# Transposed values in contiguous columns, nine stored weight blocks, two pairs coupled on TensorE, and a new order

## The chip, the cores and the metric

The kernel runs on one core of a Trainium2 chip. The metric is the device time of one execution in microseconds. One core has five engines that each run their own instruction stream: TensorE (PE, with its weight loads shown apart as PEld), VectorE (DVE), ScalarE (ACT), GpSimd (POOL) and SyncE (SP, which here does nothing but issue DMAs). Work on one engine stands in a fixed order; semaphores tie the engines together.

## The reference

Three stages follow each other. The first is a linear recurrence over 768 time steps for 4 x 8 heads of 40 x 40 state; the second and third are dense layers over 3072 tokens.

```
for t in range(768):                       # for each of 4 x 8 heads
    y[t]  = r[t] @ state
    Sa    = state @ a[t]
    state = state * w[t] - outer(Sa, b[t]) + outer(v[t], k[t])
x   = y as [3072 tokens, 320]
x2  = max(x@w1, x@w2, x@w3) @ w_out        # 320 -> 768 -> 320
out = ((x2@w_a) * (x2@w_b)) @ w_out2       # 320 -> 1536 -> 320
```

## The kernel before, in words

The recurrence is cut into 24 chunks of 32 steps; two chunks make a pair, of which there are 12 (p = 0 to 11). `prep(p)` loads a pair's inputs, forms running products of the decays (the scans at L433 and L437), scales the keys (L441), multiplies keys with the other inputs on PE (L484 for the first five pairs, L466 for the later ones, 16 matmuls of 64 columns each) and inverts the 32 x 32 triangular blocks of all heads (`solve`). The inverse is made of two 16 x 16 halves, and there are two ways to join them. For p < KS, `chain` joins them on PE: after the product with the halves (L685) come a product with the raw coupling block (L704), a copy, and a second product with the halves (L712). For p >= KS, `solve` multiplies the coupling block out beforehand on DVE and POOL (the products TC at L550 to L552), sends it through DRAM (ED, L528 and L530), and `chain` needs one product after L685 (L698). KS is 4.

`chain(c)` carries the state through chunk c and forms the chunk's outputs. For the outputs, the tile XT holds two transposed 80-row operands for 16 head pairs: the values v, loaded by DMA at L616, and the solved rows u, transposed on PE (L774) and copied by ACT at L777. The product at L786 then uses, for each of 16 index pairs, 64 columns of XT as the stationary operand and 64 columns of r (RB) as the moving one. Before the change, the 64 columns of one product stand 16 elements apart:

```
T.matmul(ps[...], XT[0:80, 2 * u + x::NU], RB[0:80, :, 2 * u + x], ...)      # L786
```

`moe_a(p)` runs the first dense stage for the 256 tokens of a finished pair (lines 909 to 938). Its weights come as 64-bit floats and are turned into two 32-bit parts (`pieces`, lines 834 to 872). `moe_b(n)` runs the second dense stage for 512 tokens (L1063 to L1073) after all chunks, six times. Its twelve weight blocks are also 64-bit. For the first LV blocks `stage_b` converts them during the recurrence and writes the parts to DRAM (WD), and `weights_b` reads them back once the recurrence's tiles are free; the rest are loaded and converted at that point (`live_b`). LV is 6.

The order is made by a planner (`Plan.run`), on the host, before the program exists. Every operation is recorded with an engine, an estimated duration, a priority and its dependences; the planner places the operation that can start first, by priority among those that are ready, and writes each engine's stream in that order. SLOPE, WP, SBP, GPR and MAP are priorities; XWAY, PMD, PME and PRE0 are latencies and margins. Where the plan leaves PE without work (between FT0 and FT1), it puts fillers into PE's stream: 128 x 128 matmuls on the identity (L313). They stand in the stream for good and run whether or not PE is idle then. The diff touches the constants, `Plan.run`, and in `body` the tile XT, its load, its copy and the product; `layout` orders v on the host.

Of the kernel before, what the change touches and what calls it, by code (L numbers as in the profile page):

```python
# [8 lines left out]
F32 = mybir.dt.float32  # L9
F32R = mybir.dt.float32r  # L10
U32 = mybir.dt.uint32
AF = mybir.ActivationFunctionType
# [3 lines left out]
B, H, S, D = 4, 8, 768, 40  # L16
C = 32
NCH = S // C
NP = NCH // 2
NU = 16  # L20
# [5 lines left out]
NACC = 9  # L26
LV = 6
KG = 5
KS = 4
NSPL = 2  # L30
DMIN = 0.4
NPB = 3
NH = 2
WP = 0.1
BIAS, BIASP = 0.2, -9
# [13 lines left out]
XRATE = 270e3  # L49
XWAY = 1.8  # L50
XISS = 0.46
XQ = 1.0
SLOPE = 0.6
PMD = 1.5
PME = 0
PRE0 = -0.5
EPA = 0.6
GPR = 0.0
SBP = 8.0
MAP = 2.0  # L60
MODE = 0.1


# [4 lines left out]
class Plan:  # L68
# [30 lines left out]
    def run(self, limit):  # L99
        n = len(self.ops)  # L100
# [6 lines left out]
        for o in reversed(self.ops):  # L107
# [3 lines left out]
            t = d + l + o["pre"] + o["xfer"]  # L111
# [15 lines left out]
        done, last, top = 0, 0, 0.0  # L127
        line, port, mode = 0.0, 0.0, None
        busy = {}

# [23 lines left out]
        while done < n:  # L154
            best = None
            for eng, rs in ready.items():
# [3 lines left out]
                c = []  # L160
                own = [est[i] for i in rs if len(self.ops[i]["ways"]) == 1] if eng == "DVE" else ()
                for i in rs:
                    o = self.ops[i]
                    s = max(ft, est[i] + o["pre"])
                    if o["xfer"]:
                        s = max(s, line - XQ)
                    if eng == "POOL" or isinstance(o["ways"][eng][0], Both):
                        s = max(s, port)
                    if o["ps"]:
                        kind = o["ps"][0][0]  # L170
                        if kind != "a" and fifo[kind][0] != i:
                            continue
                        if used.get(kind, 0) + len(o["ps"]) > limit[kind] or len(banks) < len(o["ps"]):
                            continue
                        s = max(s, heapq.nsmallest(len(o["ps"]), banks)[-1][0])
# [21 lines left out]
            s, i, eng = best  # L197
            o = self.ops[i]
            dur, fn, _ = o["ways"][eng]
            if eng == "PE":  # L200
# [30 lines left out]
                if not warm(s):  # L231
                    dur *= 2
                if o["md"] != mode:
                    dur += MODE if o["md"] else 0.0
                elif mode:
                    dur -= MODE
# [38 lines left out]
def body(nc, tc, ia, out_ap):  # L275
# [17 lines left out]
    def dma(fn, nbytes, r=(), w=(), pri=0.0, pre=1.2):  # L293
        return op("SP", XISS, fn, r=r, w=w, pri=pri, lat=XWAY, pre=pre, xfer=nbytes / XRATE)
# [57 lines left out]
    XU = ap_.tile([128, 4, 2, 40], F32, name="XU")  # L352
    XT = ap_.tile([128, 2 * C * NU], F32, name="XT")
    ZR = [ap_.tile([128, 2, 8, 2, 40], F32, name=f"ZR{i}") for i in range(NZR)]
# [237 lines left out]
    def chain(c):  # L592
# [19 lines left out]
        for g in range(2):  # L612
            r0 = GP[g]
            dma(lambda w_, g=g, r0=r0: SP.dma_start(RB[40 * g:40 * g + 40, g].rearrange("p u t -> p (u t)"), ia["rb"][c, g]),
                82e3, w=[("RB", g)], pri=pr, pre=4.0 if c else 1.2)
        dma(lambda w_: SP.dma_start(XT[0:80, 0:C * NU], ia["vt"][c]),  # L616
            260e3, w=[("XTv", 0), ("XTv", 1)], pri=pr, pre=4.0 if c else 1.2)
# [154 lines left out]
        def xtr(w_):  # L772
# [4 lines left out]
        i = op("ACT", ac(512), lambda w_: A.activation(  # L777
            XT[0:80, C * NU:2 * C * NU].rearrange("p (s n) -> p n s", n=NU), bank[w_[px]][0:80].rearrange("p (n s) -> p n s", s=32), AF.Copy),
            r=[px], w=[("XTu", 0), ("XTu", 1)], fin=[px], pri=0.2 + pr)
        pg = ("a", "g", c)  # L780

        def gmm(w_):
            ps = bank[w_[pg]]
            for u in range(8):
                for x in range(2):
                    T.matmul(ps[64 * x:64 * x + 64, u * 64:u * 64 + 64], XT[0:80, 2 * u + x::NU], RB[0:80, :, 2 * u + x], start=True, stop=True)  # L786

# [471 lines left out]
def layout(d):  # L1259
    f = np.float32  # L1260
    a6 = lambda z: np.asarray(z).reshape(B, 2, 2, 2, NCH, C, D)
    o = {}
# [30 lines left out]
    o["rb"] = np.ascontiguousarray(em(r)).reshape(NCH, 2, D, -1)  # L1293
    o["vt"] = np.ascontiguousarray(em(v).reshape(NCH, 2 * D, NU, C).transpose(0, 1, 3, 2)).reshape(NCH, 2 * D, -1)
    o["ry"] = np.ascontiguousarray(r.transpose(4, 2, 6, 0, 1, 3, 5)).reshape(NCH, 2, D, -1)
# [43 lines left out]
```

## Time and profile before

| | us |
|---|---|
| three timed runs | 1073.09, 1075.58, 1079.2 (median 1075.58) |
| the profiled execution | 1066.23, its span 1064.5 |
| PE busy in the span | 1033.2 (97%) |
| DVE, ACT, POOL busy | 611.2, 514.3, 136.8 |

The span runs from the first to the last instruction; 1.73 us of the profiled execution lie around it. A row of the groups gives a source line, engine, operation, tiles, shapes and count, then busy time, the mean of one, and the engine's idle time just before. An fp32 matmul of the program has up to two matmul records, so 768 records at L786 are 24 chunks of 16 matmuls, 448 at L466 are 14 calls, and 512 at L712 are 8 calls. A busy PE includes the fillers.

### The profile page before, as it was taken

How to read it: one execution, taken by the hardware profiler on the slowest of the kernel's cores; microseconds unless marked ns; L12 is line 12 of the kernel's file. 1: busy time of each engine (PE TensorE's matmuls, PEld its weight loads, DVE VectorE, ACT ScalarE, POOL GpSimd, SP SyncE). 2: the span in 40 equal slices, each digit the busy share in tenths (PEclk: the TensorE clock that was granted, in tenths of full speed). 3: DMA queues.
4: the chain of work that ended last, by engine and by line, in shares of the span. 5: the costliest groups of instructions: out<-in, count | busy, mean ns of one | idle time of the engine just before them, and what ended most of it. 6: DMA issues, size and time to landing. Idle time of an engine off the chain costs nothing.

```text
span 1064.5 us, 34992 instructions
## 1 busy us (share of the span) xinstructions
PE 1033.2 (97%) x15374; PEld 933.3 (88%) x15374; DVE 611.2 (57%) x1023; ACT 514.3 (48%) x1153; POOL 136.8 (13%) x124
## 2 busy tenths in 40 slices
PE   8999999899999989998999999999999999999997
PEld 8877888799989879897999999888888888888886
DVE  7966678877778767786773367673232232332222
ACT  4256886677577748575575333343232232222221
POOL 3200014221224013232120001000000000000000
PEclk9989999999999999999999999999999999999999
DMA  8744774745655465655633166512001000000000
GB/s 230 168 114 125 196 184 110 159 108 154 163 138 139 142 128 145 169 141 136 175 93 109 34 195 210 143 56 70 1 24 32 1 25 1 26 1 1 25 1 28
DMA packets 133134, 109.01 MB, mean 102 GB/s; under 512 B 90608, under 2 KB 107888, under 8 KB 132016
## 3 DMA queue, kind: packets, MB, share of 16 engines
q1 hardware_dynamic: 132112, 103.76, 37.8%
q8 instruction: 123, 2.02, 0.8%
q10 hardware_dynamic: 864, 2.95, 0.7%
q14 instruction: 35, 0.29, 0.1%
HBM read 82.15 MB, written 24.51 MB: 100 GB/s over the span
## 4 chain that ended last, share of the span: by engine, by line
PE 83%; DMA 6%; DVE 4%; ACT 3%; SPq 2%; issue 1%; POOL 1%; DVEq 0%; ACTq 0%; POOLq 0%
PE bank L1063 25%; PE bank L909 16%; PE bank L786 4%; PE bank L1071 4%; PE bank L1073 4%; PE bank L1072 4%; PE bank L804 3%; DMA KT<-in_kb_dram 2%; PE bank L645 2%; PE bank L313 2%; PE bank L934 2%; PE bank L628 2%; PE bank L738 2%; PE bank L671 1%; PE bank L935 1%; PE bank L466 1%
## 5 line engine op out<-in xcount | busy, mean ns | idle before, releaser
L1081 DVE TENSOR_TENSOR bas<-bank,bas 128x512 f32<-128x512 f32 x72 | 49.8, 691 | 201.9 <-PE bank L1063 194.7
L1063 PE MATMUL bank<-bxhi,bw 128*128 128x512 f32 x576 | 156.4, 393 | 0.0
L1063 PEld LDWEIGHTS bank<-bxhi,bw 128*128 128x128 f32 x576 | 106.3, 188 | 21.1
L1083 ACT ACTIVATE bgh<-bas 128x512 fp32r<-128x512 f32 x72 | 45.6, 633 | 130.8 <-DVE bas L1081 130.8
L1080 ACT ACTIVATE bas<-bank 128x512 f32<-128x512 f32 x72 | 43.1, 599 | 134.4 <-PE bank L1063 131.8
L909 PE MATMUL bank<-xhi,whi 128*128 128x256 f32 x432 | 94.5, 300 | 0.0
L1063 PE MATMUL bank<-bxlo,bw 128*128 128x512 f32 x288 | 89.8, 393 | 0.0
L1071 PE MATMUL bank<-bo,bgh 128*128 128x320 f32 x288 | 88.9, 309 | 0.0
L1073 PE MATMUL bank<-bo,bgl 128*128 128x320 f32 x288 | 88.9, 309 | 0.0
L1072 PE MATMUL bank<-bo,bgh 128*128 128x320 f32 x288 | 88.8, 308 | 0.0
L909 PE MATMUL bank<-xlo,whi 128*128 128x256 f32 x432 | 87.1, 283 | 0.0
L909 PE MATMUL bank<-xhi,wlo 128*128 128x256 f32 x432 | 87.1, 283 | 0.0
L924 DVE TENSOR_TENSOR hm<-bank,hm 128x512 f32<-128x512 f32 x72 | 49.5, 688 | 53.5 <-PE bank L909 50.5
L1084 DVE TENSOR_TENSOR bgl<-bas,bgh 128x512 fp32r<-128x512 f32 x72 | 49.8, 691 | 44.6 <-ACT bgh L1083 44.4
L909 PEld LDWEIGHTS bank<-xhi,whi 128*128 128x128 f32 x432 | 66.6, 191 | 2.8
L909 PEld LDWEIGHTS bank<-xhi,wlo 128*128 128x128 f32 x432 | 67.3, 192 | 0.0
L909 PEld LDWEIGHTS bank<-xlo,whi 128*128 128x128 f32 x432 | 67.2, 192 | 0.0
L313 PE MATMUL bank<-con 128*128 128x128 f32 x456 | 62.8, 292 | 3.3 <-DMA con<-in_con_dram 3.0
L1063 PEld LDWEIGHTS bank<-bxlo,bw 128*128 128x128 f32 x288 | 54.1, 188 | 12.4
L313 PEld LDWEIGHTS bank<-con 128*128 128x128 f32 x456 | 58.0, 204 | 5.6 <-ACT bank L382 2.9
L451 POOL TENSOR_TENSOR ZL<-ZL,Pp 64x512 f32<-64x512 f32 x28 | 40.0, 1429 | 175.9 <-DVE Pp L433 81.0
L909 PE MATMUL bank<-xt,wt 128*128 128x256 f32 x216 | 61.3, 284 | 0.5 <-POOL wt L872 0.5
(185 smaller groups left out, 2358.1 us busy)
## 6 DMA issues: line engine op xcount, KB each, us to landing
KT<-in_kb_dram SPq DMA_DIRECT2D x20, 384.0 KB
wraw<-in_wpb_dram SPq DMA_DIRECT2D x6, 960.0 KB
wraw<-in_wpa_dram SPq DMA_DIRECT2D x6, 768.0 KB
Wp<-in_wf_dram SPq DMA_DIRECT2D x20, 198.4 KB
ZR<-in_vz_dram SPq DMA_DIRECT2D x48, 80.0 KB
XX<-in_vx_dram SPq DMA_DIRECT2D x48, 80.0 KB
XT<-in_vt_dram SPq DMA_DIRECT2D x24, 160.0 KB
RB<-in_rb_dram SPq DMA_DIRECT2D x48, 80.0 KB
```

The source lines that it names most:

```text
L313: P.keep = lambda b: T.matmul(bank[b][:, 0:128], ident, ident, start=True, stop=True)
L786: T.matmul(ps[64 * x:64 * x + 64, u * 64:u * 64 + 64], XT[0:80, 2 * u + x::NU], RB[0:80, :, 2 * u + x], start=True, stop=True)
L909: T.matmul(ps, w, x, start=(i == 0), stop=(i == 7))
L924: op("DVE", dv(512, True), lambda w_, pn=pn: V.tensor_tensor(f(hm), bank[w_[pn]], f(hm), ALU.max), r=[pn], w=["hm"], fin=[pn], pri=ep)
L1063: T.matmul(ps, w, x, start=(k == 0), stop=(k == 7))
L1071: T.matmul(o, gh[:, c], oh, start=ff == 0, stop=False)
L1072: T.matmul(o, gh[:, c], ol, start=False, stop=False)
L1073: T.matmul(o, gl[:, c], oh, start=False, stop=ff == 11)
L1080: op("ACT", ac(512), lambda w_, j=j, pa=pa: A.activation(tb["as", j], bank[w_[pa]], AF.Copy), r=[pa], w=[("bas", j)], fin=[pa], pri=ep)
L1081: op("DVE", dv(512, True), lambda w_, j=j, pb=pb: V.tensor_tensor(tb["as", j], bank[w_[pb]], tb["as", j], ALU.mult), r=[pb], w=[("bas", j) ...
L1083: op("ACT", ac(512), lambda w_, j=j, k=k: A.activation(tb["gh", k], tb["as", j], AF.Copy), r=[("bas", j)], w=[("gh", k)], pri=ep)
L1084: op("DVE", dv(512), lambda w_, j=j, k=k: V.tensor_tensor(tb["gl", k], tb["as", j], tb["gh", k], ALU.subtract), r=[("bas", j), ("gh", k)], ...
```

## The change

XT becomes a tile [128, 16, 2, 32]: for each index pair the 32 values and the 32 solved rows lie next to each other, so the 64 columns of a product are contiguous. The host no longer transposes v, so that each row of the load, 512 contiguous elements before, now lands as 16 pieces of 32 elements (128 bytes). The copy at L777 writes runs of 32. LV goes from 6 to 9: three more weight blocks are converted during the recurrence, and three fewer after it. KS goes from 4 to 2: pairs 2 and 3 (chunks 4 to 7) get their coupling blocks from DVE and POOL. Six numbers of the planner change, and its model gets a limit on how fast PE's small matmuls are fetched.

```diff
--- before.py
+++ after.py
@@ -24,14 +24,14 @@
 NYR, NZR = 2, 1
 NW = 9
 NACC = 9
-LV = 6
+LV = 9
 KG = 5
-KS = 4
+KS = 2
 NSPL = 2
 DMIN = 0.4
 NPB = 3
 NH = 2
-WP = 0.1
+WP = 0.3
 BIAS, BIASP = 0.2, -9
 HOLD, HOLDP = {"DVE": 0.4, "POOL": 0.4}, 1
 OWN, WAIT = -9, 0.5
@@ -47,18 +47,19 @@
 LIMIT = 2.0 ** 100
 LAT = {"PE": 0.25, "ACT": 0.1, "DVE": 0.1, "POOL": 0.12}
 XRATE = 270e3
-XWAY = 1.8
+XWAY = 1.5
 XISS = 0.46
 XQ = 1.0
-SLOPE = 0.6
+SLOPE = 0.45
 PMD = 1.5
-PME = 0
+PME = 0.15
 PRE0 = -0.5
 EPA = 0.6
-GPR = 0.0
-SBP = 8.0
+GPR = 0.2
+SBP = 4.0
 MAP = 2.0
 MODE = 0.1
+ICAP, IRATE, IT = 400.0, 60.0, 40.0
 
 
 class Both(float):
@@ -126,6 +127,8 @@
                     ready.setdefault(e, set()).add(o["i"])
         done, last, top = 0, 0, 0.0
         line, port, mode = 0.0, 0.0, None
+        itime, ileft = 0.0, ICAP
+        count = lambda o: 0 if not o["md"] else 64 if o["md"] == "c64" and o["act"] > 0.42 else 128
         busy = {}
 
         state = [False]
@@ -166,6 +169,8 @@
                         s = max(s, line - XQ)
                     if eng == "POOL" or isinstance(o["ways"][eng][0], Both):
                         s = max(s, port)
+                    if eng == "PE" and o["md"] and s > IT:
+                        s = max(s, itime + (min(ICAP, count(o)) - ileft) / IRATE)
                     if o["ps"]:
                         kind = o["ps"][0][0]
                         if kind != "a" and fifo[kind][0] != i:
@@ -230,6 +235,8 @@
                         s += FD
                 if not warm(s):
                     dur *= 2
+                ileft = min(ICAP, ileft + (s - itime) * IRATE) - (count(o) or 16)
+                itime = s
                 if o["md"] != mode:
                     dur += MODE if o["md"] else 0.0
                 elif mode:
@@ -350,7 +357,7 @@
     YR = [ap_.tile([128, 2, 8, 2, 40], F32, name=f"YR{i}") for i in range(NYR)]
     XX = ap_.tile([128, 8, 2, 40], F32, name="XX")
     XU = ap_.tile([128, 4, 2, 40], F32, name="XU")
-    XT = ap_.tile([128, 2 * C * NU], F32, name="XT")
+    XT = ap_.tile([128, NU, 2, 32], F32, name="XT")
     ZR = [ap_.tile([128, 2, 8, 2, 40], F32, name=f"ZR{i}") for i in range(NZR)]
     ST = ap_.tile([128, 8, 2, 64], F32, name="ST")
     Zs = ap_.tile([128, 8, 40], F32, name="Zs")
@@ -613,7 +620,7 @@
             r0 = GP[g]
             dma(lambda w_, g=g, r0=r0: SP.dma_start(RB[40 * g:40 * g + 40, g].rearrange("p u t -> p (u t)"), ia["rb"][c, g]),
                 82e3, w=[("RB", g)], pri=pr, pre=4.0 if c else 1.2)
-        dma(lambda w_: SP.dma_start(XT[0:80, 0:C * NU], ia["vt"][c]),
+        dma(lambda w_: SP.dma_start(XT[0:80, :, 0, :], ia["vt"][c].rearrange("p (u t) -> p u t", t=32)),
             260e3, w=[("XTv", 0), ("XTv", 1)], pri=pr, pre=4.0 if c else 1.2)
         for x in range(2):
             y0 = 64 * (1 - x)
@@ -775,7 +782,7 @@
 
         op("PE", 0.4, xtr, r=["XU", "con"], w=[px], ps=[px], pri=0.2 + pr)
         i = op("ACT", ac(512), lambda w_: A.activation(
-            XT[0:80, C * NU:2 * C * NU].rearrange("p (s n) -> p n s", n=NU), bank[w_[px]][0:80].rearrange("p (n s) -> p n s", s=32), AF.Copy),
+            XT[0:80, :, 1], bank[w_[px]][0:80].rearrange("p (n s) -> p n s", s=32), AF.Copy),
             r=[px], w=[("XTu", 0), ("XTu", 1)], fin=[px], pri=0.2 + pr)
         pg = ("a", "g", c)
 
@@ -783,7 +790,7 @@
             ps = bank[w_[pg]]
             for u in range(8):
                 for x in range(2):
-                    T.matmul(ps[64 * x:64 * x + 64, u * 64:u * 64 + 64], XT[0:80, 2 * u + x::NU], RB[0:80, :, 2 * u + x], start=True, stop=True)
+                    T.matmul(ps[64 * x:64 * x + 64, u * 64:u * 64 + 64], XT[0:80, 2 * u + x].rearrange("p k s -> p (k s)"), RB[0:80, :, 2 * u + x], start=True, stop=True)
 
         op("PE", 1.08, gmm, md="c64", r=[("XTu", 0), ("XTu", 1), ("XTv", 0), ("XTv", 1), ("RB", 0), ("RB", 1)], w=[pg], ps=[pg], act=0.45, pri=0.2 + pr)
         for x in range(2):
@@ -1291,7 +1298,7 @@
     o["eye"] = np.zeros((128, 528), f)
     o["eye"][:, 16:].reshape(128, 16, 32)[:, :, 0:16] = np.eye(16, dtype=f)
     o["rb"] = np.ascontiguousarray(em(r)).reshape(NCH, 2, D, -1)
-    o["vt"] = np.ascontiguousarray(em(v).reshape(NCH, 2 * D, NU, C).transpose(0, 1, 3, 2)).reshape(NCH, 2 * D, -1)
+    o["vt"] = np.ascontiguousarray(em(v)).reshape(NCH, 2 * D, -1)
     o["ry"] = np.ascontiguousarray(r.transpose(4, 2, 6, 0, 1, 3, 5)).reshape(NCH, 2, D, -1)
     o["vx"] = np.ascontiguousarray(v.transpose(4, 2, 5, 0, 1, 3, 6)).reshape(NCH, 2, C, -1)
     o["vz"] = np.ascontiguousarray(v[:, :, ::-1].transpose(4, 3, 5, 0, 1, 2, 6)).reshape(NCH, 2, C, -1)
```

The lines of `before` below L47 stand 7 further down afterwards (L786 is L793, L313 is L320).

PE, chunk 4, the first of pair 2, in the stream before: the product with the halves, the coupling product (L704) and the second product with the halves (L712), with the dense stage's L909 between them.

```order
L685 MATMUL bank_67<-Zs,TT_142 32x40 x32
L909 MATMUL bank_65<-xhi,whi 128x256 x2
...
L909 MATMUL bank_65<-xl_110,wt_103 128x256
L704 MATMUL bank_66<-Zy,NB_145 32x40 x32
L909 MATMUL bank_69<-xhi,whi 128x256 x2
...
L909 MATMUL bank_69<-xl_110,wt_103 128x256
L712 MATMUL bank_67<-Zs,TT_142 32x40 x32
```

The same place in the stream after: the product with the halves, then one product with the finished coupling block (L705).

```order
L692 MATMUL bank_66<-Zs,TT_142 32x40 x32
L916 MATMUL bank_63<-xhi,whi 128x256 x2
...
L916 MATMUL bank_63<-xl_110,wt_103 128x256
L916 MATMUL bank_63<-xhi,whi 128x256 x2
...
L916 MATMUL bank_63<-xl_110,wt_103 128x256
L705 MATMUL bank_70<-Zy,NB_145 32x40 x32
```

The third product (L712, L719 after) is gone from chunks 4 to 7.

PE, where pair 4's key products (L484) stand in chunk 6, before: 12 fillers behind the second one, then the key transposes (L628).

```order
L804 MATMUL bank_67<-YL,YR_133 40x32 x32
L484 MATMUL bank_65<-ZL_128,KT_125 64x32 x32
L313 MATMUL bank_67<-con 128x128 x12
L628 MATMUL bank_67<-con,KT_126 128x104 x4
L628 MATMUL bank_65<-con,KT_126 128x104 x4
L313 MATMUL bank_64<-con 128x128 x2
```

The same pair after: 34 fillers (L320) between its two key products (L491), and 8 ahead of the product with the halves.

```order
L635 MATMUL bank_64<-con,KT_126 128x104 x4
L635 MATMUL bank_69<-con,KT_126 128x104 x4
L320 MATMUL bank_63<-con 128x128 x8
L692 MATMUL bank_63<-Zs,TT_140 32x40 x32
L491 MATMUL bank_64<-ZL_128,KT_125 64x32 x32
L320 MATMUL bank_69<-con 128x128 x34
L491 MATMUL bank_69<-ZL_128,KT_125 64x32 x32
```

Over the whole stream the fillers go from 228 to 269: 197 before and 250 after stand ahead of the eighth product at L786 (of chunk 7), 31 and 19 behind it.

SP, the loads of pair 2's coupling blocks (NB) and of one chunk's values (XT), before: NB comes straight from BD, the values as 80 x 512.

```order
L512 DMA NB_145<-BD_73 16x16x16
L609 DMA XX<-in_vx_dram 32x640 x2
L616 DMA XT<-in_vt_dram 80x512
L609 DMA ZR_137<-in_vz_dram 32x640 x2
L614 DMA RB<-in_rb_dram 40x512 x2
```

SP, the same pair after: the values as 80 x 16 x 32, and NB by way of TC and ED.

```order
L530 DMA TT_142<-TD_76 32x16x32 x4
L623 DMA XT<-in_vt_dram 80x16x32
L621 DMA RB<-in_rb_dram 40x512 x2
L427 DMA ZL_128<-in_aa_dram 48x2x512
L535 DMA ED_79<-TC 64x128 x2
L427 DMA ZL_128<-in_aa_dram 48x2x512
L627 DMA YL<-in_ry_dram 40x512 x2
L537 DMA NB_145<-ED_79 16x16x16 x3
```

The load of the values keeps its place among a chunk's loads; NB of pairs 2 and 3 moves behind the end of that pair's inverse.

## Rows read from the trace of the kernel before

**Rows 1.** The page, part 4: chain that ended last, share of the span by engine

```profile
PE 83%; DMA 6%; DVE 4%; ACT 3%; SPq 2%; issue 1%; POOL 1%; DVEq 0%; ACTq 0%; POOLq 0%
```

**Rows 2.** Stretches: start:end, length, busy us (count) of PE, PEld, DVE, ACT, POOL; clock, DMA, GB/s

```profile
0.00:73.00 73.00, 68.18 (x1076) 61.88 (x1078) 58.43 (x91) 28.91 (x73) 16.95 (x18) 0.95 0.69 173
73.00:170.00 97.00, 94.99 (x2542) 78.20 (x2543) 67.59 (x116) 71.88 (x184) 7.74 (x11) 0.96 0.64 160
170.00:260.00 90.00, 86.59 (x2044) 79.18 (x2032) 71.06 (x123) 66.49 (x161) 26.18 (x24) 1.00 0.58 139
260.00:605.00 345.00, 330.02 (x7214) 310.53 (x7214) 238.98 (x401) 217.75 (x509) 80.04 (x62) 0.99 0.51 133
605.00:664.00 59.00, 59.00 (x496) 58.83 (x495) 37.80 (x73) 20.25 (x41) 4.11 (x7) 1.00 0.63 186
664.00:1064.50 400.50, 394.38 (x2034) 344.72 (x2032) 137.31 (x222) 108.98 (x188) 1.84 (x2) 1.00 0.10 29
```

**Rows 3.** Waits of PE: line, what it waited for, us in total, times, longest us

```profile
PE bank L466 <- DVE KT L441: 5.8, 2, 4.1
PE bank L804 <- DVE YL L790: 3.6, 1, 3.6
PE bank L738 <- issue: 2.7, 3, 1.2
PE bank L786 <- ACT XT L777: 1.7, 8, 0.3
```

**Rows 4.** Groups on PE by line and shape: count, busy us, mean ns, idle before

```profile
L786 PE MATMUL bank<-RB,XT 80*64 80x64 f32 x768 | 50.1, 283 | 1.7 <-ACT XT L777 1.7
L786 PEld LDWEIGHTS bank<-RB,XT 80*64 80x64 f32 x768 | 46.8, 211 | 5.2 <-ACT XT L777 3.3 <-issue 0.3
L466 PE MATMUL bank<-ZL,KT 128*64 128x64 f32 x448 | 16.6, 230 | 6.3 <-DVE KT L441 5.8 <-issue 0.5
L466 PEld LDWEIGHTS bank<-ZL,KT 128*64 128x64 f32 x448 | 14.8, 143 | 8.4 <-issue 7.0 <-ACT YR L635 0.5
L712 PE MATMUL bank<-Zs,TT 32*32 32x40 f32 x512 | 7.1, 207 | 0.6 <-issue 0.6
L313 PE MATMUL bank<-con 128*128 128x128 f32 x456 | 62.8, 292 | 3.3 <-DMA con<-in_con_dram 3.0 <-ACT YR L656 0.4
```

**Rows 5.** The same view, lines on ACT, DVE and POOL

```profile
L777 ACT ACTIVATE XT<-bank 80x512 f32<-80x512 f32 x24 | 25.5, 1062 | 16.4 <-PE bank L774 14.4 <-DVE ST L757 1.8
L922 ACT ACTIVATE hm<-bank 128x512 f32<-128x512 f32 x36 | 21.6, 599 | 36.2 <-PE bank L909 30.5 <-POOL hlo L926 1.9 <-DVE hlo L927 1.9
L837 DVE SCALAR_TENSOR_TENSOR wraw<-wraw,wca 128x960 f32<-128x960 uint32 x6 | 6.9, 1146 | 0.0
L552 DVE TENSOR_REDUCE TC<-TP 128x64 f32<-128x512 f32 x8 | 5.4, 675 | 0.0
L550 POOL TENSOR_TENSOR TP<-BU,TU 128x512 f32<-128x512 f32 x16 | 21.9, 1385 | 64.9 <-ACT TU L586 62.4 <-DVE TC L552 2.5
```

**Rows 6.** The page, parts 2 and 3: DMA packets by size, and the main queue

```profile
DMA packets 133134, 109.01 MB, mean 102 GB/s; under 512 B 90608, under 2 KB 107888, under 8 KB 132016
q1 hardware_dynamic: 132112, 103.76, 37.8%
```

**Rows 7.** Timeline of the SP queue around one load of the values: start us, us

```profile
217.25 2.01 SPq L616 DMA_DIRECT2D XT<-in_vt_dram  x1
```

**Rows 8.** Timeline of PE, the product that needs that load: start us, us

```profile
226.69 2.05 PE L786 MATMUL bank<-RB,XT 80*64 80x64 f32 x32
```

**Rows 9.** The chain of waits around 290 us: start us, us, what

```profile
285.95 7.02 DMA KT<-in_kb_dram
293.07 1.24 DVE KT L441
294.39 1.15 PE bank L466 x32
```

## The prediction

> **What bounds the kernel now.** I began with the chain of waits as shares by engine [rows 1]: TensorE holds 83% of what ended last, DMA 6%, VectorE 4%, ScalarE 3%. The kernel is bound by TensorE's own stream, so any microsecond taken out of that stream should show nearly whole. The view by stretches [rows 2] says where. Up to 605 us the chunks run, from 605 to 664 us the first dense stage ends, and from 664 us the second dense stage runs alone. In the last stretch TensorE does 394.38 us of work in 400.5 us, and nothing in its matmuls is edited, so 400 us of the span are fixed. Ahead of it TensorE is busy 68.18 + 94.99 + 86.59 + 330.02 + 59.00 = 638.8 of 664 us; only 25 us are idle. VectorE is busy 58.43 of 73, 67.59 of 97, 71.06 of 90 and 238.98 of 345 us: high in the first 260 us, 69% later. The third view, TensorE's waits [rows 3], names little: 5.8 us in two waits for scaled keys (L441), 3.6 us for one mask, 2.7 us of issue, and 1.7 us in eight waits for the copy into XT. Others wait for TensorE far more: a single copy line, L922, stood idle 30.5 us for L909 [rows 5]. The fourth view, the groups [rows 4], shows what in TensorE's stream is dear.
>
> **The product on XT.** L786 has 768 records in 50.1 us: 24 calls of 50.1 / 24 = 2.09 us [rows 4]. L466 has the same 16 matmuls of 64 stationary and 64 moving columns, with contiguous stationary columns: 16.6 / 14 = 1.19 us a call. Their weight loads differ likewise, 211 against 143 ns. The matmuls' moving operands are laid out alike (two runs of 32), only the rows differ (80 against 128), and I take it that fewer rows don't make a product slower. So the spread columns are the cause, and contiguous ones give 24 x (2.09 - 1.19) = 24 x 0.90 = 21.6 us back. The bounds are 0 (the cause is another) and 24 x (2.09 - 1.15) = 22.6 us (one L466 call on the chain took 1.15 [rows 9]). I take 21.6.
>
> A rule of the Trainium skill speaks against it: "TensorE: Matmul & The Clock Gate", section "LDWEIGHTS (loading the stationary operand)", has a load's time follow from the number of columns alone, and both lines load 64; by that rule this term would be 0. The trace does not agree with it here, 211 against 143 ns at equal columns. "SBUF — State Buffer", section "Door 1: The DMA port swizzle (why `[64,N]` ≈ `[32,N]`)", says that fp32 accesses more than four elements apart pay for each new line, and the elements here stand 16 apart; with it the trace agrees.
>
> **The copy into XT.** L777 takes 1062 ns and writes single elements 64 bytes apart; L922 copies as many columns in 599 ns into contiguous space [rows 5]. The copy should drop to about 0.6 us, 24 x 0.46 = 11 us of ScalarE. ScalarE is not the bound; what reaches TensorE is at most the 1.7 us of the eight waits [rows 3]. I count 0 to 1.7 and take 0.
>
> **The load of the values.** 24 loads of 80 rows become 24 x 1280 pieces. The main queue's 132112 packets took 37.8% of 16 engines' 1064.5 us [rows 6], which is 6438 us or 48.7 ns a packet on the mean. A load then takes 1280 x 48.7 / 16 = 3.9 us instead of 0.9 (160 KB at the 186 GB/s of the fifth stretch [rows 2]). The net 28800 packets are 28800 x 48.7 / 16 = 88 us of all 16 engines, which lifts their share ahead of 605 us from a weighted mean of 0.56 [rows 2] by 0.15. The loads have room: one was issued at 217.25 us and its product began at 226.69 us [rows 7, 8], 9.4 us later. Its cost at TensorE is 0 with that cover, and up to 24 x 3.0 = 72 us if it is gone everywhere; near the first row I take 0.
>
> **Three more stored blocks.** Each is converted in six passes over 128 x 960; the longest kind takes 1.15 us [rows 5], so at most 6.9 us a block and 20.7 us for three, on VectorE or in part on GpSimd, moved from behind 605 us to ahead of it. It lands in the later chunks, where VectorE goes from 69% to at most (238.98 + 20.7) / 345 = 75%. Behind 605 us VectorE loses as much, where TensorE never waited: 59.00 of 59 us busy. The bytes read after the recurrence stay the same (stored parts are as long as the raw 64-bit block). Cost 0, covered by TensorE's own work; without cover up to 20.7. I take 0, since VectorE's idle time there is 106 us.
>
> **Coupling of pairs 2 and 3.** Four chunks lose L712, 7.1 / 8 = 0.89 us a call [rows 4]: 4 x 0.89 = 3.6 us out of TensorE's stream. In exchange each pair gets three products and three sums over 512 elements: 0.675 us a sum, and 0.675 to 1.385 us a product by engine [rows 5], 3 x 1.35 to 3 x 2.06 = 4.1 to 6.2 us a pair, in the first 260 us where VectorE is busiest. Its coupling block now waits for TC and a trip through ED. Behind the ED store on SP's queue stand a load of the next pair's inputs, the loads of r and the weights of the first dense stage; behind L698 on TensorE stand the state update and all that follows. The plan puts fillers there, and these are the price I count.
>
> **Fillers.** The streams hold 228 before and 269 after. L313 was busy 62.8 us, 62.8 / 228 = 0.275 us each, so 41 more cost 11.3 us. Twelve fewer stand behind chunk 7 and 53 more ahead of it; there they take 14.6 us of what the first chunks gain. They run whether needed or not, so 11.3 is firm unless they stand where TensorE would have waited anyway, which the waits [rows 3] show for 25 us at most.
>
> **The rest of the order.** It can take back some of the 25 us of waits or add to them. A faster L786 leaves the other engines less lead. The nearest row is the pair of waits for scaled keys, 5.8 us. Bounds: -12 (half of all idle goes) to +15 (each of ten pairs waits 1.5 us more). I take +3, half of that row.
>
> **Sum.** -21.6 - 3.6 + 11.3 + 3 = -10.9. The profiled execution is 1066.2 us, 9.4 us under the median of the runs; I take the difference as the same on either, so 1066.2 - 10.9 = 1055.3 there and 1075.6 - 10.9 = 1064.7 by the median. I forecast 1064.5.
>
> **Rivals.** *All of it arrives.* The new order takes waits back as well: -21.6 - 3.6 + 11.3 - 12 = -26, 1050. For it: the planner counts L786 as long as L466, so the order before was made for a faster product than the chip had, and now fits. Against: TensorE has only 25 us of idle to win.
>
> *The first chunks eat it.* Up to 260 us VectorE runs at up to 80% (58.43 of 73, then 71.06 of 90) [rows 2], and takes 8 to 12 us of new products; the 53 fillers mark where the plan itself sees TensorE wait. If these chunks lengthen by the whole 12 us, -10.9 + 12 = +1, 1076: no change. Against: VectorE's work there is hidden wherever dense work fills TensorE.
>
> *The DMA engines become the bound (slower).* The place is the keys' load. In the chain it landed 7.02 us after issue, the scaling followed at once and TensorE's L466 right behind it [rows 9], so what delays that load delays TensorE. The load of the values, 3.9 us of all engines, goes through the same queue in every chunk. If it pushes the keys' load of all ten later pairs back by 3.0 us, it costs 30 us: -10.9 + 30 = +19, 1095; if of half, 15: 1080. It decides from 11 us on, about 1.1 us a pair. For it: the share is 0.69 and 0.64 in the first stretches. Against: only two of ten pairs waited for keys. "DMA: Bandwidth & Descriptors", section "Specifications", of the Trainium skill puts the piece for full rate at 512 bytes or more; the pieces are 128. That 90608 of 133134 packets are under 512 bytes already [rows 6] agrees with pieces being usual here, and no run yet shows their price.
>
> *The change doesn't do what it says.* If L786 stays at 2.09 us for another reason, nothing gives the other engines less lead either, and the sum is -3.6 + 11.3 = +7.7, 1083. For it only that the rows differ, against it two like products in one trace. The rule on columns cited above would have it so.
>
> **How the numbers follow.** Forecast 0.50 (its own range 1058 to 1070), all arrives 0.20 (1046 to 1058), first chunks 0.15 (1070 to 1081), DMA 0.11 (1080 to 1095), no effect 0.04. The range that should hold 8 of 10 reaches from 1047 to 1080. What a measurement here can tell from no change is 0.5%, 5.4 us: faster is under 1070.2, same up to 1081. Faster: nearly all of the forecast, 0.48, the second case 0.20 and a little of the third 0.02, 0.70. Same: 0.13 + 0.02 + 0.02 = 0.17. Slower: 0.13.
>
> **What would show it.** In the profile after, L793 (the old L786) at about 28.5 us in all and its weight loads near 143 ns; L784 (the old L777) near 0.6 us; fillers at 74 us; L719 with 256 records; waits of TensorE under 30 us ahead of the second dense stage, which starts 10 us or so earlier and lasts as long. I am wrong if L793 keeps 2 us a call, if waits for keys, for XT or for coupling blocks grow past 15 us together, or if the granted clock, 0.95 and 0.96 in the first two stretches, falls in the later ones.

## Result: 2.6% faster, some two and a half times the forecast gain

The changed kernel takes 1044.66 us (median of four runs, 1041.81 to 1049.88); the kernel before, run beside it, 1074.93 (four runs, 1073.09 to 1079.2). The ratio on record is 0.9736, with an interval of 0.9697 to 0.9775 (the two medians alone give 0.972). Forecast were 1064.5 and a range of 1047 to 1080. The profiled execution of the changed kernel took 1043.9 us, span 1042.0, mean granted clock 0.995; that of the kernel before 1066.23, 1064.5 and 0.989.

In the profile after, first the page: busy time by engine, DMA packets by size, the main queue, and the chain's shares.

```profile
span 1042.0 us, 34646 instructions
PE 1011.2 (97%) x15200; PEld 913.6 (88%) x15200; DVE 623.5 (60%) x1014; ACT 501.7 (48%) x1143; POOL 140.8 (14%) x115
...
DMA packets 165180, 115.01 MB, mean 110 GB/s; under 512 B 121632, under 2 KB 140704, under 8 KB 164064
...
q1 hardware_dynamic: 163728, 108.31, 42.0%
...
PE 90%; DMA 3%; ACT 2%; DVE 2%; issue 2%; POOL 1%; SPq 1%; POOLq 0%; DVEq 0%
```

TensorE is bound as before, its share of the chain higher (83% in [rows 1]). Its busy time fell by 22.0 us, its idle time by 0.5 (1064.5 - 1033.2 = 31.3 to 1042.0 - 1011.2 = 30.8): the span's 22.5 us lie in busy time.

The groups of the changed lines (busy us, mean ns of one, then idle time before them) show in which:

```profile
L320 PE MATMUL bank<-con 128*128 128x128 f32 x538 | 70.8, 285 | 5.9 <-DMA con<-in_con_dram 2.9 <-ACT Zs L684 1.6 <-DVE YL L797 0.7
...
L793 PE MATMUL bank<-RB,XT 80*64 80x64 f32 x768 | 28.0, 225 | 0.5 <-issue 0.5
L793 PEld LDWEIGHTS bank<-RB,XT 80*64 80x64 f32 x768 | 24.6, 138 | 3.4 <-issue 0.7
...
L784 ACT ACTIVATE XT<-bank 80x512 f32<-80x512 f32 x24 | 14.3, 594 | 13.0 <-PE bank L781 12.2 <-ACT YR L642 0.5
...
L719 PE MATMUL bank<-Zs,TT 32*32 32x40 f32 x256 | 3.2, 199 | 0.0
```

The product (L793, L786 before) went from 50.1 to 28.0 us and its weight loads from 211 to 138 ns [rows 4]; the copy into XT from 1062 to 594 ns [rows 5]; the third products (L719, L712 before) from 7.1 to 3.2 us. The 269 fillers (538 records) take 70.8 us instead of 62.8. That is -22.1 - 3.9 + 8.0 = -18.0 of the 22.0 us.

The remaining 4 us can't be put down to a line: busy times of neighbouring groups overlap, and the other groups together fall by 1.6 us only. The stretches show what else differs. The columns are those of [rows 2]; the last but two is the granted clock.

```profile
0.00:73.00 73.00, 69.92 (x1247) 62.59 (x1248) 62.20 (x100) 32.36 (x84) 15.35 (x17) 1.00 0.75 185
73.00:170.00 97.00, 92.95 (x2396) 77.16 (x2394) 75.89 (x125) 75.85 (x196) 19.61 (x17) 1.00 0.66 162
170.00:260.00 90.00, 88.73 (x1940) 82.98 (x1942) 81.58 (x126) 60.32 (x151) 33.28 (x27) 1.00 0.64 144
260.00:589.00 329.00, 312.99 (x7161) 294.18 (x7159) 247.16 (x414) 210.87 (x503) 71.20 (x54) 0.99 0.61 151
589.00:642.00 53.00, 53.00 (x441) 52.70 (x441) 19.55 (x34) 13.36 (x24) 0.00 (x0) 1.00 0.78 226
642.00:1042.00 400.00, 393.59 (x2029) 343.99 (x2028) 137.12 (x220) 108.90 (x188) 1.31 (x1) 1.00 0.10 28
```

Where [rows 2] had a granted clock of 0.95 and 0.96 in the first two stretches, it is 1.00 now. The second dense stage is the same 400 us and begins 22 us earlier, where some 10 were forecast.

**Time and clock apart.** Each run lists its mean granted clock. The runs of the kernel before spread with it: over 40 of them, a line through time against clock falls by 9.0 us for each 0.01 of clock. Time multiplied by clock (below: the net time) is thus a fair reading of what the kernel would take at full clock, and time less net of what it loses to the clock. It is an estimate, good to some 2 us over a difference of 0.01, where it takes 10.7 us and the line 9.0; it counts a low clock as lost even while TensorE waits, where it costs nothing. It shows already that the profile I worked from, at 0.989, was a fast execution of the kernel before; its other runs had 0.983 on the mean.

### The profile page after: what moved, and what is told of

Same layout as the page of the kernel before. It is cut to its first block, busy times and chain, and to the rows that moved or that the text cites. A ratio compares the mean times of both kernels' runs of the same rounds, so it can differ in the third digit from the quotient of the medians.

```text
span 1042.0 us, 34646 instructions
## 1 busy us (share of the span) xinstructions
PE 1011.2 (97%) x15200; PEld 913.6 (88%) x15200; DVE 623.5 (60%) x1014; ACT 501.7 (48%) x1143; POOL 140.8 (14%) x115
## 4 chain that ended last, share of the span: by engine, by line
PE 90%; DMA 3%; ACT 2%; DVE 2%; issue 2%; POOL 1%; SPq 1%; POOLq 0%; DVEq 0%
PE bank L1070 26%; PE bank L916 18%; PE bank L320 6%; PE bank L1080 4%; PE bank L1078 4%; PE bank L1079 4%; PE bank L811 3%; PE bank L793 2%; PE bank L491 2%; DMA KT<-in_kb_dram 2%; PE bank L941 2%; PE bank L652 2%; PE bank L635 2%; PE bank L942 2%; PE bank L678 2%
## 5 line engine op out<-in xcount | busy, mean ns | idle before, releaser
L320 PE MATMUL bank<-con 128*128 128x128 f32 x538 | 70.8, 285 | 5.9 <-DMA con<-in_con_dram 2.9
L320 PEld LDWEIGHTS bank<-con 128*128 128x128 f32 x538 | 65.3, 197 | 9.9 <-ACT bank L389 2.9
L916 PE MATMUL bank<-xl,wt 128*128 128x256 f32 x216 | 61.0, 282 | 0.0
```

What stands on the lines that cost most here:

```text
L320: P.keep = lambda b: T.matmul(bank[b][:, 0:128], ident, ident, start=True, stop=True)
L916: T.matmul(ps, w, x, start=(i == 0), stop=(i == 7))
```

## The experiments

Ratios are to the kernel before, run in the same session (medians 1070.8 in the first session, 1070.5 in the second, 1072.1 in the third; net 1053.3, 1053.6 and 1054.4, lost 16 to 18). They are as recorded, not quotients of the medians shown. The clock is the mean of a kernel's runs, net and lost are medians. The changed kernel ran only in the session of the result, four times, beside a kernel before at 1074.9; so its differences in us from the other versions go across sessions, and the ratios decide. "The rest" means everything but the layout of XT.

| kernel | us | ratio and interval | clock | net | lost | fillers |
|---|---|---|---|---|---|---|
| before | 1070.8 | 1 | 0.984 | 1053.3 | 16.0 | 228 |
| after | 1044.7 | 0.9736 [0.9697, 0.9775] | 0.993 | 1038.9 | 6.3 | 269 |
| layout alone | 1060.0 | 0.9906 [0.9877, 0.9936] | 0.978 | 1036.8 | 22.3 | 228 |
| the rest alone | 1059.3 | 0.9909 [0.9873, 0.9944] | 0.994 | 1054.1 | 6.4 | 269 |
| after, long pieces | 1042.3 | 0.9732 [0.9696, 0.9769] | 0.995 | 1036.4 | 5.2 | 269 |
| after, old planner numbers | 1053.4 | 0.9862 [0.9816, 0.9908] | 0.987 | 1040.7 | 13.2 | 273 |
| layout and KS 2 | 1055.8 | 0.9868 [0.9803, 0.9933] | 0.989 | 1044.4 | 11.1 | 290 |
| layout and LV 9 | 1080.6 | 1.0083 [1.0037, 1.0129] | 0.977 | 1055.7 | 24.2 | 282 |
| after, 48 fillers out | 1048.9 | 0.9802 [0.9721, 0.9884] | 0.986 | 1033.8 | 15.3 | 221 |
| after, 117 fillers out | 1053.2 | 0.984 [0.9778, 0.9903] | 0.972 | 1023.2 | 29.5 | 152 |
| after, KS 4 | 1050.7 | 0.9783 [0.9725, 0.9842] | 0.985 | 1035.8 | 14.2 | 244 |
| after, PME 0 | 1050.7 | 0.9788 [0.973, 0.9846] | 0.989 | 1039.1 | 11.6 | 271 |
| after, TPH 250 | 1047.4 | 0.976 [0.9711, 0.9809] | 0.993 | 1038.8 | 6.3 | 291 |
| after, PMD 3 | 1058.1 | 0.9873 [0.981, 0.9936] | 0.985 | 1042.6 | 15.4 | 290 |

### Layout alone

The kernel before with XT's new tile, load, copy, product and host order, and nothing else.

```diff
-    XT = ap_.tile([128, 2 * C * NU], F32, name="XT")
+    XT = ap_.tile([128, NU, 2, 32], F32, name="XT")
-        dma(lambda w_: SP.dma_start(XT[0:80, 0:C * NU], ia["vt"][c]),
+        dma(lambda w_: SP.dma_start(XT[0:80, :, 0, :], ia["vt"][c].rearrange("p (u t) -> p u t", t=32)),
-     T.matmul(..., XT[0:80, 2 * u + x::NU], RB[0:80, :, 2 * u + x], ...)
+     T.matmul(..., XT[0:80, 2 * u + x].rearrange("p k s -> p (k s)"), RB[0:80, :, 2 * u + x], ...)
```

> The kernel before with contiguous columns in XT alone (tile, load, copy, product); order, stored blocks and coupled pairs stay. Theory: the product falls from 2.09 to about 1.17 us a call, TensorE's busy time by 22 us, and the time by 18 to 23 us (about 1053), the rest of the change owing the other 7 to 12 us of the measured 30. Rival 1, that the layout owes all of it because an order planned for a fast product now fits: 1045 to 1048. Rival 2, that the old order turns the time into waits: above 1060, with waits of TensorE over 40 us where there were 31.

It took 1060.0, where about 1053 was expected. From its profile, busy time by engine, then its product among the groups, then TensorE's longest waits (us in total, times, longest):

```profile
span 1061.0 us, 34993 instructions
...
PE 1023.2 (96%) x15374; PEld 922.5 (87%) x15374; DVE 610.1 (58%) x1023; ACT 504.5 (48%) x1153; POOL 136.3 (13%) x124
```

```profile
L786 PE MATMUL bank<-RB,XT 80*64 80x64 f32 x768 | 28.5, 229 | 0.0
```

```profile
PE bank L466 <- DVE KT L441: 6.3, 2, 4.5
...
PE bank L804 <- DVE YL L790: 3.7, 1, 3.7
```

The product gave its whole 21.6 us. But TensorE's idle time rose from 31.3 to 37.8 us, and the clock fell: 0.978 on the mean, against 0.984. Net of the clock the layout gave 1053.3 - 1036.8 = 16.5 us, and 6.3 us of that went to the clock. Stretches of its span show what stood ahead of a low clock:

```profile
120.00:130.00 10.00, 8.89 (x188) 7.42 (x182) 3.27 (x5) 5.38 (x13) 0.00 (x0) 0.75 0.47 127
130.00:140.00 10.00, 10.00 (x166) 9.11 (x166) 5.31 (x8) 5.82 (x15) 1.95 (x2) 0.50 0.67 173
140.00:150.00 10.00, 10.00 (x250) 7.94 (x251) 5.71 (x9) 4.56 (x14) 0.00 (x0) 0.73 0.38 82
```

TensorE stood idle for 1.1 us, then the clock fell to 0.50 (1.2 GHz, half of its upper level), and in the middle row 166 matmuls fill ten microseconds. A busy 10.00 there is slow work, not more work.

### The rest alone

The changed kernel with XT spread as before.

```diff
-    XT = ap_.tile([128, NU, 2, 32], F32, name="XT")
+    XT = ap_.tile([128, 2 * C * NU], F32, name="XT")
     (load, copy, product and host order of the kernel before)
```

> The kernel after with spread columns in XT again; order, nine blocks and two coupled pairs as after. Theory: the product is back at 2.09 us a call and the time 20 to 24 us above the kernel after, 1065 to 1069, so 6 to 10 us under the kernel before, with a granted clock above 0.99. Rival 1 (the layout owes all): 1073 to 1077, no different from before. My sum on record for the rest alone was +10.7 (fillers 11.3, third products -3.6, waits +3): 1086.

It took 1059.3, a gain of 11.5 us, where 1065 to 1069 was expected; my sum on record had it as a loss, 1086. Busy time by engine and the product's group in its profile:

```profile
span 1053.0 us, 34643 instructions
...
PE 1029.3 (98%) x15200; PEld 932.6 (89%) x15200; DVE 625.1 (59%) x1014; ACT 511.8 (49%) x1143; POOL 139.5 (13%) x115
```

```profile
L793 PE MATMUL bank<-RB,XT 80*64 80x64 f32 x768 | 50.3, 283 | 0.9 <-ACT XT L784 0.9
```

This profile ran at a clock of 0.999, with no stretch of ten microseconds under 1.00 ahead of its last three, so it needs no correction: 1054.8 us, 1.5 above the net 1053.3 of the kernel before. The rest gains next to nothing in work, in spite of 41 more fillers; of its 11.5 us the clock explains 9.6 by this estimate, 6.4 lost instead of 16.0. The idle time is 1053.0 - 1029.3 = 23.7 us, 7.6 under that of before.

With the layout on top, this order goes to the 1042.0 us of the changed kernel: -22.3 for the product, +7.1 idle (23.7 to 30.8), and +4.2 in other busy lines, near the 3.4 us that this profile, at 0.995, loses to the clock: -11.0. So the layout's product gives 22 us and takes 7 back as waits in either order (6.5 in the old one), and 15 to 16 remain.

### Long pieces

The changed kernel, with the values loaded in one 2 KB piece a row into a half of XT that isn't read; the product takes its 64 contiguous columns from the solved rows. The values are left out of the result.

```diff
-    XT = ap_.tile([128, NU, 2, 32], F32, name="XT")
+    XT = ap_.tile([128, 2, NU * 32], F32, name="XT")
-        SP.dma_start(XT[0:80, :, 0, :], ia["vt"][c].rearrange("p (u t) -> p u t", t=32))
+        SP.dma_start(XT[0:80, 0], ia["vt"][c])
```

> The kernel after, the values loaded as one piece of 2 KB a row into a half of XT that the product does not read (it reads 64 contiguous columns of the solved rows, so the values are left out of the result). Theory: the short pieces cost nothing at TensorE, so the time stays within 0.3% of the kernel after (1042 to 1048), while packets fall by some 29000 and the main queue's share by 3 to 8 points. Rival, that the queue delays the keys: 5 us or more faster than the kernel after, and waits for scaled keys and halves (7 us after) gone.

```profile
DMA packets 136380, 115.01 MB, mean 110 GB/s; under 512 B 90912, under 2 KB 109984, under 8 KB 135264
...
q1 hardware_dynamic: 134928, 108.31, 40.1%
```

It took 1042.3, with 28,800 packets fewer, as counted beforehand. The intervals of the two ratios nearly coincide, 0.9732 [0.9696, 0.9769] against 0.9736 [0.9697, 0.9775]: 128-byte pieces cost at most some 6 us here (the two half intervals taken together), and nothing that can be told from 0. The DMA engines are not the bound. The queue's share fell by 1.9 points only, where 3 to 8 were expected: 42.0% of 16 x 1042.0 us less 40.1% of 16 x 1045.6 us is some 290 us, so each packet more took about 10 ns of an engine, not the 48.7 of the prediction.

### Old planner numbers

The changed kernel's layout, KS and LV, planned with the old numbers.

```diff
-WP = 0.3          XWAY = 1.5   SLOPE = 0.45   PME = 0.15   GPR = 0.2   SBP = 4.0   IT = 40.0
+WP = 0.1          XWAY = 1.8   SLOPE = 0.6    PME = 0      GPR = 0.0   SBP = 8.0   IT = 1e9
```

> Contiguous columns, nine stored blocks and two coupled pairs, but the planner's numbers of the kernel before and no limit on fetching. Theory: the new order owes most of what the layout does not, so this is 5 to 10 us slower than the kernel after, 1050 to 1055. Rival, that the blocks and the pairs owe it: within 3 us of the kernel after.

1053.4: the numbers are worth 9 us in medians. The net time is 1040.7 against 1038.9; 7 of the 9 us are clock. (With IT alone set back in the changed kernel, the planner writes the same streams, so there the limit on fetching changes nothing.)

### Two pairs, and three blocks, on the layout alone

```diff
-KS = 4
+KS = 2            # one kernel
-LV = 6
+LV = 9            # the other
```

> The kernel before with contiguous columns and two pairs coupled on TensorE instead of four (six stored blocks, the old planner numbers). Theory now: net of the clock the layout gives -15, and what the rest gives is clock; I expect the pairs to owe a good part of it, since the lost clock lay in chunks 0 to 7: granted clock 0.984 to 0.988 where layout alone has 0.979, time 1052 to 1056. Rival, that the planner's numbers owe all of it: 0.979 and 1058 to 1062.

> The kernel before with contiguous columns and nine stored blocks (four pairs on TensorE, old planner numbers). Theory: the blocks are hidden and change neither work on TensorE nor its clock by themselves: 1056 to 1062 at 0.977 to 0.982. Rival, that a busier VectorE delays TensorE: above 1064.

With KS 2 alone it took 1055.8. The net time is worse than that of the layout alone (1044.4 against 1036.8, with 62 more fillers), the clock better (11.1 lost against 22.3). With LV 9 alone it took 1080.6, where 1056 to 1062 was expected. Its profile says where, busy time first, then the fillers:

```profile
span 1076.8 us, 35199 instructions
...
PE 1034.4 (96%) x15482; PEld 933.8 (87%) x15482; DVE 609.1 (57%) x994; ACT 502.5 (47%) x1141; POOL 142.4 (13%) x123
```

```profile
L313 PE MATMUL bank<-con 128*128 128x128 f32 x564 | 75.6, 289 | 4.4 <-DMA con<-in_con_dram 2.9 <-DVE XY L808 0.8 <-ACT Zy L689 0.6
```

The rival named a busier VectorE, and the time is in its range, above 1064. VectorE's whole busy time (609.1, 610.1 with the layout alone) can't decide, since the conversions only move to an earlier place. Between 260 and 605 us VectorE is busier, as the stretches of the layout alone, then of this kernel, show:

```profile
260.00:605.00 345.00, 327.53 (x7495) 307.99 (x7493) 245.25 (x421) 219.65 (x531) 81.34 (x63) 0.99 0.57 137
260.00:605.00 345.00, 324.38 (x7165) 304.67 (x7164) 259.94 (x431) 219.07 (x523) 88.31 (x70) 0.99 0.62 152
```

But TensorE's waits that end on VectorE are shorter, 6.0 us in all against 11.8 (sums over the view of waits), so no direct delay by VectorE shows. TensorE has 54 more fillers (75.6 us, 11 more than with the layout alone), 4.6 us more idle time (42.4), and still loses 24.2 us to the clock: here the fillers bought nothing. Why the planner makes so poor an order of it with the old numbers stays open.

### Fillers taken out

The changed kernel without the 48 fillers between the 6th and the 7th product on XT, and without all but the first 152.

```diff
-    P.keep = lambda b: T.matmul(bank[b][:, 0:128], ident, ident, start=True, stop=True)
+    P.keep = lambda b: None if 202 <= next(kept) < 250 else T.matmul(...)    # 48 out
+    P.keep = lambda b: None if next(kept) >= 152 else T.matmul(...)          # 117 out
```

> The kernel after without the 48 fillers between its sixth and seventh product L793; all else stands as it did. They are 48 x 0.263 = 12.6 us of TensorE. Theory now: they stand where TensorE would wait for the keys of pair 4, and hold the clock; without them waits grow by 5 to 10 us, the clock falls there, and the time is within 5 us of the kernel after (1040 to 1050). My sum on record (each filler costs its 0.275 us): 1031 to 1033.

> The kernel after with only the first 152 fillers (ahead of the first product); the other 117, 117 x 0.263 = 30.8 us, are gone. Theory now (fillers hold the clock and fill real waits): the granted clock falls to 0.98 or less in the first 200 us and the time rises, 1045 to 1055. My sum on record (they cost what they take): 1014 to 1018. A third reading, that waits replace them one for one and the clock holds: 1042 to 1046.

Both came out slower than the changed kernel, 1048.9 and 1053.2. For the second the intervals of the ratios lie apart; for the first they overlap, so that it is slower is not shown by the times alone. With 30.8 us of fillers less, the kernel took longer. The place shows in TensorE's timeline, with VectorE's scaling of the keys of pair 4 (L448) from its own timeline (start, us, line, count, idle before), in the changed kernel:

```profile
165.44 1.83 PE L320 MATMUL bank<-con 128*128 128x128 f32 x14 [1.01 <-ACT Zs L684]
...
173.63 2.05 PE L320 MATMUL bank<-con 128*128 128x128 f32 x16
...
176.44 2.06 PE L491 MATMUL bank<-ZL,KT 40*64 40x32 f32 x64
178.42 7.86 PE L320 MATMUL bank<-con 128*128 128x128 f32 x68
186.21 2.33 PE L491 MATMUL bank<-ZL,KT 40*64 40x32 f32 x64
```

```profile
184.53 1.19 DVE L448 TENSOR_TENSOR KT<-KT,Rr 128x1024 f32<-128x1024 f32 x1
```

and in the one with 48 fillers out, whose lines are one further down:

```profile
174.53 0.79 PE L693 MATMUL bank<-Zs,TT 32*32 32x40 f32 x64 [1.44 <-DVE XY L816]
...
176.24 3.41 PE L492 MATMUL bank<-ZL,KT 40*64 40x32 f32 x58 [0.42 <-issue]
185.57 0.39 PE L492 MATMUL bank<-ZL,KT 40*64 40x32 f32 x2 [5.92 <-DVE KT L449]
186.20 3.62 PE L492 MATMUL bank<-ZL,KT 40*64 40x32 f32 x62 [0.24 <-DVE ZL L461]
```

```profile
184.23 1.19 DVE L449 TENSOR_TENSOR KT<-KT,Rr 128x1024 f32<-128x1024 f32 x1
```

The keys are ready at 185.72 us in the one and 185.42 in the other. Ahead of that the first has 7.86 us of fillers; without them TensorE waits 5.92 us and gets nowhere sooner (the next products start at 186.21 and 186.20). What differs comes behind: 62 of the same 64 matmuls take 3.62 us, where all took 2.33. In stretches, the changed kernel first, then the other:

```profile
170.00:186.00 16.00, 16.00 (x295) 15.56 (x296) 14.58 (x17) 6.01 (x17) 4.26 (x3) 1.00 0.76 144
```

```profile
170.00:175.00 5.00, 2.86 (x124) 2.51 (x126) 4.89 (x7) 3.90 (x13) 3.21 (x2) 1.00 0.85 187
175.00:180.00 5.00, 4.22 (x100) 3.90 (x86) 4.83 (x9) 2.87 (x8) 0.79 (x1) 0.54 0.23 57
180.00:186.00 6.00, 0.39 (x2) 0.28 (x2) 5.91 (x6) 0.54 (x2) 1.15 (x1) 0.50 1.04 175
186.00:192.00 6.00, 5.80 (x72) 5.74 (x73) 4.92 (x12) 2.51 (x8) 2.47 (x4) 0.50 0.45 59
192.00:200.00 8.00, 8.00 (x181) 7.63 (x180) 5.78 (x8) 5.03 (x12) 1.25 (x1) 0.97 0.55 165
```

With the fillers the clock held at 1.00 throughout. Without them it had fallen before the long wait began at 179.65 us: the 48 fillers include those at 170 to 175.6 us, TensorE was idle for 2.14 of the five microseconds up to 175, in short waits (the longest 1.44 us), and then the clock went to 0.50. It stayed there across the wait of 5.92 us and came back during the last stretch, which is busy throughout. A wait was not always followed by a fall: the changed kernel waits 1.01 us ahead of 165.44, and the clock stays at 1.00.

By the table, 48 fillers cost 1038.9 - 1033.8 = 5.1 us net and keep 15.3 - 6.3 = 9.0 us of clock; 117 cost 15.7 and keep 23.2. That is 0.11 to 0.13 us of cost and 0.19 to 0.20 us of clock for each. Both are upper bounds: in the two profiles without them 3.3 and 4.2 us of the lost clock lie in waits of TensorE, where it costs nothing, so some 2 us of cost and 6 of clock for the 48, 11 and 19 for the 117, are nearer (an estimate from one profile each).

The kernel before shows a like place in its first stretch, 1.74 us idle and then a low clock:

```profile
50.00:60.00 10.00, 8.26 (x162) 5.92 (x161) 9.48 (x22) 5.15 (x16) 2.81 (x2) 0.93 0.54 149
60.00:70.00 10.00, 10.00 (x226) 9.40 (x226) 4.90 (x8) 4.91 (x11) 0.00 (x0) 0.73 0.40 108
```

Over the ten-microsecond stretches under 0.995 up to 1030 us, the lost time sums to 10.2 us in the profile before, and to 3.4 us in the profile after, where two are left, 330 to 340 and 380 to 390 us, both 0.83.

### One number of the changed kernel at a time

```diff
-KS = 2            # first kernel
+KS = 4
-PME = 0.15        # second
+PME = 0
-NPH, TPH, HKE = 4, 130.0, 0.45      # third
+NPH, TPH, HKE = 4, 250.0, 0.45
-PMD = 1.5         # fourth
+PMD = 3.0
```

> The kernel after with four pairs coupled on TensorE again (KS = 4), planned with the new numbers: 244 fillers where the kernel after has 269. Theory (the clock in the first chunks is what the pairs, the fillers and the new numbers buy together): a granted clock between 0.984 and 0.990, net of the clock 1036 to 1042, time 1049 to 1057. Rival, that the new numbers alone keep the clock: 0.993 or more and 1041 to 1047.

> The kernel after without the margin on results that TensorE waits for (PME = 0), 271 fillers. Theory: the margin is one of the numbers that let the plan see TensorE's gaps; without it the clock loses 0.003 to 0.006 and the time is 1046 to 1052. Rival, that it is of no account: 1041 to 1047 at 0.993.

> The kernel after with the denser check for fillers kept up to 250 us instead of 130 (TPH = 250): 291 fillers, 22 more, at 0.13 to 0.26 us each net of the clock (3 to 6 us). Theory: little clock is lost between 130 and 250 us in the kernel after, so they buy little: 1043 to 1050. Rival, that more fillers still pay as the earlier ones did: 1036 to 1041, a version that beats both.

> The kernel after planned with a margin of 3.0 us, not 1.5, on loads that TensorE waits for (PMD = 3), 290 fillers. Theory: the two waits for keys near 330 and 380 us, with the half clock behind them, are loads that land later than planned; with the margin they shrink and the clock reaches 0.996 or more, but 21 more fillers cost 3 to 6 us: 1040 to 1047. Rival: the order moves elsewhere and the waits with it, 1047 to 1056.

KS 4 and PME 0 both took 1050.7, 6 us more (5 to 6 by the ratios, whose intervals overlap that of the changed kernel), with net times no worse than the changed kernel's (1035.8 and 1039.1): each takes back a part of the clock, 14.2 and 11.6 us lost, as expected. TPH 250 lets the planner place fillers over a longer stretch, 22 more of them: 1047.4, net and lost as in the changed kernel, no gain. PMD 3 has the planner count on later data. It was meant for the two waits for keys that are left; the chain of the changed kernel shows both (start, us, what), here the second:

```profile
376.09 6.47 DMA KT<-in_kb_dram
...
382.72 2.18 POOL KT L448
...
384.94 1.09 PE bank L473 x29
```

It took 1058.1, above the 1040 to 1047 expected and above its rival. Stretches of its profile show that the two waits went, and that TensorE runs dry elsewhere instead:

```profile
240.00:250.00 10.00, 7.01 (x84) 6.52 (x82) 4.27 (x4) 2.22 (x3) 2.62 (x1) 0.92 0.23 68
...
330.00:340.00 10.00, 10.00 (x196) 9.64 (x195) 9.41 (x14) 4.68 (x10) 4.32 (x2) 1.00 0.65 170
380.00:390.00 10.00, 10.00 (x329) 9.08 (x329) 8.47 (x19) 8.53 (x21) 0.45 (x1) 1.00 0.63 170
```

Over its runs it loses 15.4 us to the clock; the profiled one, at 0.993 and 1050.96 us, was the fastest, so it doesn't show all of where the others lose it. No version came out faster than the changed kernel beyond the measurement.

## Why the prediction was wrong, point by point

- **The product on XT**, -21.6: right, -22.1. The rule on columns in "TensorE: Matmul & The Clock Gate", section "LDWEIGHTS (loading the stationary operand)", of the Trainium skill does not hold here: 64 columns loaded in 211 ns spread and 138 to 141 ns contiguous, in two orders. The case that the change does nothing falls with it.
- **The copy**, 0.46 us each and nothing in the end: right in size, 1062 to 594 ns.
- **The load of the values**, 0: right within 6 us. The DMA rival needed 11 us and is refuted. Its price was mis-sized: 48.7 ns, the mean of all packets, was taken for each short one, which took about 10, so a load takes some 0.8 us more (1200 x 10 / 16), not 3.0.
- **Coupling of two pairs**, -3.6: right as work, -3.9. That it also changes the clock was not in it.
- **Three more stored blocks**, 0: no loss seen in the new order (the rest alone is at most 1.5 us slower at full clock), though LV alone was not set back there, so its own price is not shown. On the old numbers they came with 20 us, as fillers, waits and clock, none of which that step had.
- **Fillers**, +11.3 and called firm: this step failed. In busy time they took 8.0 us more, as one took 0.263 us instead of 0.275. What they add to the time is less, since half or more of them stand where TensorE would have waited, the exception that the step itself named: at most 0.11 to 0.13 us each, or 5 us for 41. Above all they are not only a cost: they hold the clock across waits, and with 117 of them taken out the kernel was slower.
- **The rest of the order**, +3: -0.5, the sum of two that I had not parted: the layout added about 7 us of waits in either order (a shorter product leaves less cover, as the prediction feared), the rest removed 7.6.
- **The sum**, -10.9: it has no term for the granted clock, and that is the step that decided. Net of the clock the change gives 1053.3 - 1038.9 = 14.4 us, 3.5 more than the sum. The clock gives 16.0 - 6.3 = 9.7 more. These 24 us stand against 26 to 30 us between the medians, by session. The rows were there: [rows 2] with 0.95, 0.96 and 0.99 means 0.05 x 73 + 0.04 x 97 + 0.01 x 345 = 11 us that a steady clock could return. I named a falling clock as a way to be wrong and never priced a rising one. For the same reason the step from the profiled execution to the median was wrong, "the same on either": the profile before, at 0.989, lost less than that kernel usually does, so the gain is larger by the medians (30) than by the profiles (22).

Of the rivals, *all of it arrives* named the nearest time, 1050, but for another reason: it had the order win back 12 us of waits, and it won back 0.5, and 9.7 us of clock. *The first chunks eat it* did not happen: VectorE is busier there (81.58 of 90 us, 71.06 before), but the eighth product on XT, of chunk 7, begins at 215.39 us, 11.3 earlier than before [rows 8]:

```profile
215.39 1.15 PE L793 MATMUL bank<-RB,XT 80*64 80x64 f32 x32
```

What stays open is which edit buys how much of the clock. The layout in the old order loses 22.3 us, the rest in either layout 6.4. With KS, PME or all the old numbers put back it is 11.6 to 14.2, so they do not add up, and each order has its own few places where TensorE runs dry.

## What to carry to other kernels

Read the granted clock as a term of the sum: one minus the clock, times the stretch, is time that an order can win or lose, and a profile at a better clock than the other runs understates it. Work placed in a wait has a price only for the part that outlasts the wait, and may pay for itself in the clock of the work behind it; so price a filler by where it stands, not by its duration. A shortened step returns less than its own time when it covered waits: here 22 us became 15.

## What was not expected of the hardware

- The stride of the stationary columns alone, 64 bytes against contiguous, costs 73 ns a weight load of 64 columns (211 to 138) and 0.9 us a call of 16 matmuls.
- With 48 fillers taken out, TensorE was idle for 2.14 of five microseconds in short waits, and the granted clock then fell from 1.00 to 0.50; it was still there behind a further wait of 5.92 us, where 62 matmuls took 3.62 us and 64 had taken 2.33.
- Loading the values in pieces of 128 bytes, 28,800 packets more (the main queue's share is 42.0% with them, 40.1% without), cost nothing that could be measured, within some 6 us.
